# An S5 scan and a dilated local attention on one core: skip term and scan sums copied into PSUM by ScalarE, a pair level in the chunk scan, four taps per attention operation, and a new order of all work

## The chip, the core and the metric

The kernel runs on one core of one Trainium2 chip. The core has a matrix engine (TensorE, PE in the profile; its weight loads are shown apart as PEld), a vector engine (VectorE, DVE), an engine for copies and functions (ScalarE, ACT), a general one (GpSimd, POOL) and one that issues transfers (SyncE, SP). Matmuls read from the on-chip memory SBUF and write to, or add to, the accumulators in PSUM, eight banks of 512 float32 columns on 128 partitions in the way this kernel uses it. The time is the device time of one run in microseconds (us), the median of three runs.

## The reference

Two independent computations on sequences of S = 2048 positions and D = 448 channels; their results stand side by side in the output, 896 columns wide.

```python
# A: a diagonal state-space model (S5), complex state of 448
dt = jnp.exp(log_dt)
Lam_bar = jnp.exp(dt * Lam)
B_bar = ((Lam_bar - 1.0) / Lam)[:, None] * Bmat
Bu = jnp.einsum("bld,pd->blp", x + 0j, B_bar)
for t in range(L):
    h = Lam_bar[None, :] * h + Bu[:, t, :]
    hs.append(h)
y = 2.0 * jnp.einsum("blp,dp->bld", hseq, Cmat).real + x * Dskip[None, None, :]
# B: attention of 16 heads of 28 channels over 8 earlier positions, 2 apart
qkv = (x @ wqkv) ...                        # q, k, v
idx = pos[:, None] - jnp.arange(8) * 2      # positions below 0 are masked
logits = jnp.einsum("bhsd,bhswd->bhsw", q, kg) * scale
attn = _softmax(logits, axis=-1)
o = jnp.einsum("bhsw,bhswd->bhsd", attn, vg)
b = o.reshape(B, S, D) @ wo
```

Inputs and outputs are bfloat16.

## The kernel before

*Layout.* The 2048 positions are 128 chunks of T = 16. A chunk is a partition in position-major tiles and a column in transposed ones; a position j inside the chunk picks the tile.

*How the order is made.* Every piece of work is a unit (`P.add`) with an engine, a cost, the units it depends on, and the buffers it takes and gives back: two PSUM slots `W` of two banks, four slots `s` of one bank, three product buffers `PR`, and smaller rings. `Planner.run` could order them by cost and priority (`PRI`), but a list `ORDER` of 606 numbers replaces that: the units are issued in exactly that order. Each engine works through its own instructions in the order issued, and waits by semaphore where a unit depends on another engine.

*Part A, the scan.* The state is cut into 7 groups m of 128 rows (64 complex numbers as real and imaginary parts). For each group `scan` does the following, with up to three groups in flight:
- The inputs: matmuls of the transposed x with `Bcat` for the four residues i = j mod 4, each 512 columns (L1192, L1200). Residues 0 and 2 lie in the two banks of `scP`, 1 and 3 in `scb` tiles.
- ACT copies `scP` to `eP` (L1205). Matmuls with the power `L(1)` carry residue 0 to 1 and 2 to 3 (L1209), ACT copies `scb1` to `e1` (L1213), L(2) carries 1 to 3 (L1216), ACT copies (L1220), and L1224 to L1226 sum the four quarters of a chunk. Now the last 128 columns of `scb3` hold each chunk's total.
- The scan over 128 chunks, four levels. In each, ACT copies the 128 totals to `pbuf` (`evv`, L1229) and matmuls of 128 columns add the totals of earlier chunks (`l2`, L1234): 1, 2, 3 chunks back, then 4, 8, 12, then 16, 32, 48, then 64: ten matmuls. A fifth copy is the input of what follows.
- The way back: L1239 adds the carry to residue 3, ACT writes it to `h` (`ev3`, L1243). Residues 1, 0 and 2 left PSUM long ago, because their banks were wanted by the next group. So an identity matmul brings `e1` back into a PSUM slot (`back1`, L1252, in six groups), L1246 and L1247 add the carries, ACT copies it out (`ev1f`, L1258); two identity matmuls bring `eP` back (`back`, L1263, in five groups), carries are added, then L1269, and ACT copies it out (`evPf`, L1274). Where `PRI["h.."]` or `PRI["g.."]` is positive the banks are held instead: `eP` in groups 3 and 6, `e1` in group 6.

*Part A, the outputs.* For each pair of positions a `y_ps` slot `W` takes, per position, seven matmuls of 448 columns with `Ccat` (L1356). The skip term x * Dskip comes in two ways: for the first six pairs as four more matmuls per position (L1353) against a diagonal matrix `Dg`, which ACT builds at the start (L1101) from a transposed row of Dskip; for the last two pairs DVE multiplies positions 12 to 15 of x, loaded again, by Dskip (L1333) and adds them while it takes y out of PSUM (L1367). The first six pairs are taken out by ACT (L1365).

*Part B.* x is transposed partly by PE (L413) and partly by transfers; matmuls make q and k (L466, L473, L499), taken out by ACT and DVE (L201 to L207). DVE multiplies q with shifted k (L641, L645, into `prods`), PE sums over the channels of a head (L656, L662, `logits`). `softmax`: maximum on DVE (L684), subtracted by PE (L688), exponential on ACT (L694), sum by PE (L699), reciprocal and product on DVE (L703, L705), transposed by PE (L711) and copied by ACT in two halves (L716). Values come from L741 and lie in `vd`. Then `pv`, for four quarters of the positions in the order (1,1), (1,0), (0,1), (0,0): an operation on DVE multiplies two neighbouring taps of the values by their weights (L797, 3584 elements a partition, four of them), three adds (L800, or L812 in two parts in the last quarter) and a fold of the two halves (L809; the last quarter leaves it to PE). The partial sums live in `rb`, the products in `prods`. For three quarters a transfer transposes the result; the last one is transposed by PE (L849) and taken out by ACT (L854). `wo_ps` (L866) is the output projection, taken out in L201, and L205 for a part of one tile.

Of the kernel before, what the change touches and what calls it, by code (L numbers as in the profile page):

```python
# [34 lines left out]
KPOW = [1, 2, 4, 8, 12, 16, 32, 48, 64, 128, 192, 256, 512, 768, 1024]  # L35
# [4 lines left out]
WARM = 4  # L40
FILL = (1, 3)
PRI = dict(bm=-5.66, xa=2.77, cc=19.9, sc=2.9, ch=-27.35, bk=-0.56, v0=16.0, v1=-26.16, wo=-13.74, y=14.16, pw=-5.68, sm=13.48, lim=100.0, lim2=30.0, limv=70.0, qk=0.86, K11=-14.0, Q11=-13.0, K10=-12.0, Q10=-11.0, K01=-10.0, Q01=-9.0, K00=-8.0, Q00=-7.0, d3=10.94, h0=-1.0, g0=-1.0, h1=-1.0, g1=-1.0, h2=-1.0, g2=-1.0, h3=1.0, g3=-1.0, h4=-1.0, g4=-1.0, h5=-1.0, g5=-1.0, h6=1.0, g6=1.0, nd=4.0, xd=20.12)
ORDER = [
# [51 lines left out]
class Unit:  # L95
    __slots__ = ("eng", "cost", "fn", "deps", "prio", "acq", "rel", "lat", "end", "seq", "on", "until", "mode")


class Planner:


    def __init__(self, bufs):
        self.units = []
        self.free = {k: [0.0] * n for k, n in bufs.items()}

    def add(self, eng, cost, fn, deps=(), prio=0.0, acq=None, rel=None, lat=None, until=None,
            mode="f"):
        u = Unit()
        u.mode = mode
        u.eng = eng if isinstance(eng, tuple) else (eng,)  # L110
        u.cost = cost if isinstance(cost, tuple) else (cost,)
        u.fn, u.prio, u.rel, u.until = fn, prio, rel, until
        u.acq = () if acq is None else (acq,) if isinstance(acq, str) else acq
# [4 lines left out]
        return u  # L118

    def run(self):  # L120
        left = list(self.units)
        nwait = {id(u): len({id(d) for d in u.deps}) for u in left}
        users = {}
        for u in left:
            for d in {id(d): d for d in u.deps}.values():
                users.setdefault(id(d), []).append(u)
        ready = [u for u in left if not nwait[id(u)]]
        clock = {}
        order = []
        n = len(left)  # L130
        mode = "f"
        while len(order) < n:
            best = None
            for u in ready:
                if any(len(self.free[a]) < u.acq.count(a) for a in u.acq):
                    continue
                for eng, cost in zip(u.eng, u.cost):
# [3 lines left out]
                    for a in u.acq:  # L141
                        t = max(t, sorted(self.free[a])[u.acq.count(a) - 1])
                    if u.until is not None and eng == u.eng[-1] and t > u.until:
                        continue
                    key = (t, u.prio, u.seq, t)
                    if best is None or key < best[0]:
                        best = (key, u, eng, cost + (0.095 if eng == "PE" and u.mode != mode else 0.0))
            assert best, "no unit can start: %d left, waiting for %s" % (n - len(order), [(u.acq, u.fn.__qualname__) for u in ready])
            (_, _, _, t), u, eng, cost = best
            for a in u.acq:  # L150
                self.free[a].remove(min(self.free[a]))
# [5 lines left out]
            for a in (u.rel,) if isinstance(u.rel, str) else u.rel or ():  # L157
                self.free[a].append(u.end)
# [5 lines left out]
            order.append((t, u, cost))  # L164
        self.order = order
        if len(ORDER) == n:
            for i in ORDER:
                u = self.units[i % 1000]
                u.on = u.eng[i // 1000]
# [1317 lines left out]
```

## Time and profile before

The profile is of one execution. The trace's span is 140.4 us; what lies around it is in the runs' times but not in the span.

| what | us |
|---|---|
| median of 3 runs | 142.12 (142.12, 142.16, 141.61) |
| span of the profiled execution | 140.4 |
| PE busy | 134.9 |
| DVE busy | 120.9 |
| ACT busy | 93.6 |
| POOL busy | 21.1 |
| first product of q and k on DVE starts | 15.48 |
| first operation of `pv` on DVE starts | 66.98 |
| first y matmul on PE starts | 101.19 |
| last add of `pv` on DVE ends | 131.3 |
| last matmul ends | 137.0 |

The busy time of an engine is the time in which at least one of its instructions was running. Idle time on an engine counts only where something waits for that engine later. In the rows of groups, the first number is the busy time of the group, the second the mean length of one instruction in nanoseconds; matmuls overlap in that length, so the distance from one to the next is smaller and is read from the chain of waits, where "x4" is four matmuls in a row and the number before it their time together. The values in the slices of the clock are tenths of full speed.

### The profile page before, as it was taken

Reading aid. Unit: us, or ns where it says so; the run is one execution under the profiler, and the core shown is the slowest. Engines: PE = TensorE matmul, PEld = TensorE weight load, DVE = VectorE, ACT = ScalarE, POOL = GpSimd, SP = SyncE. Lnnn points to the kernel's source line nnn. Section 1 sums busy time; section 2 is a strip of 40 time slices with the busy share of each in tenths; the row PEclk is TensorE's granted clock in tenths of the full one; section 3 lists DMA queues with packets and bytes.
Section 4 is the critical chain, followed back from the end, with each engine's and each line's share of the span. In section 5 each row is a group of like instructions: output and inputs, shape, how many; then the busy total and the mean of one; then the engine's idle time right before and its main releaser. Section 6 shows DMA issues by size and latency. Waiting matters only on the chain.

```text
span 140.4 us, 2813 instructions
## 1 busy us (share of the span) xinstructions
PE 134.9 (96%) x1078; PEld 71.6 (51%) x1078; DVE 120.9 (86%) x128; ACT 93.6 (67%) x182; POOL 21.1 (15%) x68
## 2 busy tenths in 40 slices
PE   5999999999999999999999999999999999999990
PEld 1634333456554454666435554456655555555650
DVE  3245959999999989897998999999999999999931
ACT  3358879999765883578776789889873630551381
POOL 7374287000970000000000000000000000000000
PEclk9999999999999999999999999999999999999999
DMA  4965243996537616469999400600154155724044
GB/s 129 267 120 111 56 100 56 238 218 123 81 67 76 103 42 203 110 94 175 248 199 142 144 0 5 131 0 0 35 101 132 47 181 139 170 80 139 0 161 133
DMA packets 39390, 15.99 MB, mean 114 GB/s; under 512 B 31445, under 2 KB 38740, under 8 KB 39377
## 3 DMA queue, kind: packets, MB, share of 16 engines
q1 hardware_dynamic: 39314, 15.82, 50.6%
q8 instruction: 8, 0.13, 0.4%
q14 instruction: 5, 0.04, 0.1%
q10 hardware_dynamic: 63, 0.01, 0.0%
HBM read 4.27 MB, written 3.67 MB: 57 GB/s over the span
## 4 chain that ended last, share of the span: by engine, by line
PE 94%; DMA 2%; ACT 1%; issue 0%; DVE 0%; ACTq 0%
PE y_ps L1356 15%; PE qk_ps L466 12%; PE v_ps L741 9%; PE wo_ps L866 9%; PE scb L1192 7%; PE scP L1192 7%; PE logits L656 4%; PE scb L1234 3%; PE qk_ps L499 3%; PE qk_ps L473 2%; DMA ra<-in_B_x_dram 2%; PE scb L1209 2%; PE y_ps L1353 2%; PE scP L1200 2%; PE scP L1263 2%; PE pt_x L413 1%
## 5 line engine op out<-in xcount | busy, mean ns | idle before, releaser
L797 DVE TENSOR_TENSOR prods<-attn,vd 128x3584 bf16<-128x3584 bf16 x12 | 24.0, 2020 | 0.0
L641 DVE TENSOR_TENSOR prods<-qk 128x3072 bf16<-128x3072 bf16 (+1 forms) x17 | 22.8, 1379 | 1.0 <-PE logits L656 0.5
L800 DVE TENSOR_TENSOR rb<-rb,prods 128x3584 bf16<-128x3584 bf16 x11 | 22.2, 2022 | 0.1
L466 PE MATMUL qk_ps<-rb 128*128 128x512 bf16 x60 | 15.3, 386 | 0.0
L1356 PE MATMUL y_ps<-Ccat,qk 128*128 128x448 bf16 x64 | 14.9, 352 | 0.0
L866 PE MATMUL wo_ps<-wo_p,rb 128*128 128x448 bf16 x64 | 13.5, 352 | 0.0
L741 PE MATMUL v_ps<-rb 128*128 128x448 bf16 x64 | 13.1, 352 | 0.0
L1229 ACT CAST pbuf<-scb 128x128 bf16<-128x128 f32 x35 | 9.2, 272 | 4.9 <-PE scb L1234 4.3
L1192 PEld LDWEIGHTS <-Bcat 128*128 128x128 bf16 x84 | 7.6, 98 | 8.2 <-issue 1.9
L1356 PE MATMUL y_ps<-Ccat,h 128*128 128x448 bf16 x48 | 11.7, 353 | 0.0
L1365 ACT CAST qk<-y_ps 128x896 bf16<-128x896 f32 x6 | 5.4, 907 | 9.1 <-PE y_ps L1356 9.1
L201 ACT CAST qk<-wo_ps 128x448 bf16<-128x448 f32 (+1 forms) x16 | 8.3, 526 | 4.2 <-PE wo_ps L866 3.9
L1192 PE MATMUL scb<-xaT_sb,Bcat 128*128 128x512 bf16 x42 | 11.1, 380 | 0.0
L1192 PE MATMUL scP<-xaT_sb,Bcat 128*128 128x512 bf16 x42 | 10.9, 379 | 0.0
L201 ACT CAST qk<-qk_ps 128x512 bf16<-128x512 f32 (+2 forms) x14 | 7.8, 580 | 2.9 <-PE qk_ps L473 1.2
L203 ACT ACTIVATE qk<-qk_ps 128x512 bf16<-128x512 f32 (+1 forms) x16 | 9.3, 599 | 0.5 <-PE qk_ps L499 0.2
L466 PEld LDWEIGHTS <-rb 128*128 128x128 bf16 x60 | 5.8, 100 | 7.4 <-issue 1.2
L201 ACT CAST vd<-v_ps 128x448 bf16<-128x448 f32 x16 | 7.9, 542 | 2.5 <-PE v_ps L741 2.5
L1356 PEld LDWEIGHTS <-qk 128*128 128x128 bf16 x64 | 6.3, 98 | 5.8
L645 DVE TENSOR_TENSOR prods<-qk 128x768 bf16<-128x768 bf16 (+3 forms) x18 | 9.1, 569 | 0.1
L741 PEld LDWEIGHTS <-rb 128*128 128x128 bf16 x64 | 6.1, 98 | 5.3
L866 PEld LDWEIGHTS <-rb 128*128 128x128 bf16 x64 | 6.1, 98 | 5.0
(177 smaller groups left out, 251.9 us busy)
## 6 DMA issues: line engine op xcount, KB each, us to landing
out_dram<-qk SPq DMA_DIRECT2D x18, 112.0 KB, 1.7
out_dram<-qk SPq DMA_DIRECT2D x7, 224.0 KB, 2.2
vd<-vd SPq DMA_DIRECT2D x3, 392.0 KB
rb<-in_B_wqkv_dram SPq DMA_DIRECT2D x3, 336.0 KB
qk<-in_A_x_dram SPq DMA_DIRECT2D x1, 448.0 KB
ra<-in_A_B_re_dram SPq DMA_DIRECT2D x1, 392.0 KB
ra<-in_A_B_im_dram SPq DMA_DIRECT2D x1, 392.0 KB
rb<-in_A_C_re_dram SPq DMA_DIRECT2D x4, 98.0 KB
```

The source lines that it names most:

```text
L201: nc.scalar.copy(out, in_)
L203: nc.scalar.mul(out, in_, scale)
L466: nc.tensor.matmul(out(n), lhsT=w(n, full, k), rhs=self.xT[:, j:j + 4, k, :], start=(not rfirst and k == 1), stop=(rfirst and k == KT - 1) ...
L641: V.tensor_tensor(out.rearrange("p i j k q -> p i (j k) q"), qq.unsqueeze(1).to_broadcast([NCH, 2, 4 * nk, NCH]), bass.AP(kk.tensor, kk.of ...
L645: V.tensor_tensor(jk(out[:, i, a:e]), qq, kk, op=ALU.mult)
L741: nc.tensor.matmul(ps[:].rearrange("p h d -> p (h d)"), lhsT=self.xT[:, j, k, :], rhs=self.wv[:, k, :], start=(k == 0), stop=(k == KT - 1))
L797: V.tensor_tensor(tmp[i].rearrange("p (j d h) -> p j d h", j=8, d=DH), aa, self.vd[:, o:o + 8], op=ALU.mult)
L800: V.tensor_tensor(acc, acc, tmp[i], op=ALU.add)
L866: nc.tensor.matmul(ps[:], lhsT=o[:, kt, :], rhs=self.wo_p[:, KT * e + kt, :], start=(kt == 0), stop=(kt == KT - 1))
L1192: mt(box[i], lhsT=self.Bcat[:, k, m, :], rhs=self.xk(slice(i, None, 4), k), start=(i % 2 == 0 and k == 0), stop=False, **kw)
L1229: nc.scalar.copy(pb[:, dst, PAD:], box[3][:, 384:512])
L1356: nc.tensor.matmul(ps, lhsT=self.h[m][:, i, g * NCH:(g + 1) * NCH], rhs=self.Ccat[:, m, :], start=(m == 0 and not skip), stop=(m == NM - 1 ...
```

## The change

It has six parts.

1. *Skip term.* The matmuls with `Dg`, `Dg` itself and the transposed row of Dskip are gone. All of x is loaded again, in position-major form, in four transfers of four positions each, into the tile that held the transposed x (so after the last input matmul of the scan, `self.u_in`). DVE multiplies each by Dskip; ACT copies each pair into a y slot (`seed`) before the seven matmuls add to it; y is then a plain copy out, by ACT or DVE.
2. *Scan sums.* In `back1` and `back`, ACT copies `e1` and `eP` into the PSUM slot instead of identity matmuls, in the same groups (`FIN`: "seed" or "hold" for `eP` and `e1`).
3. *Pair level.* The chunk scan first adds each even chunk to the odd one after it, then runs three levels over the 64 odd chunks (2, 4, 6; 8, 16, 24; 32, 64, 96 chunks back), then adds the odd chunks to the even ones: 11 matmuls of 64 columns with five copies of 64 columns, and one of 128 at the end.
4. *Attention values.* An operation takes four taps (7168 elements): two multiplies and one add for a quarter. Both buffers, T1 and T2, lie in the product buffer `prods`, now 2 x 7168 long, so that the first multiply waits until the last logits have been summed.
5. *Softmax.* The reciprocal becomes a logarithm and an exponential on ACT; the transposed weights are copied by one operation instead of two.
6. *Front, buffers and order.* The k weights are loaded in two pieces; some copies change engines; the planner now knows which PSUM slot a unit takes (`Slot`), and keeps some for some uses; `ORDER` is a new list of 622 numbers, in which also some y and wo tiles are taken out by DVE after its last attention operation.

```diff
@@ scan: the way back
-            def back1(box=box):
-                t = self.psum.tile([NCH, 512], f32, name="scb1", tag="s")
-                box[1] = t[:]
-                mt(box[1], lhsT=cx.ident[:], rhs=box["e1"][:], start=True, stop=False, **kw)
+            def back1(eng, box=box, sl=sl, m1=m1):
+                box[1] = self.psum.tile([NCH, 512], f32, name="scb1", slot=sl["b1"])[:]
+                if eng == "ACT":
+                    nc.scalar.copy(box[1], box["e1"][:])
+                else:
+                    mt(box[1], lhsT=cx.ident[:], rhs=box["e1"][:], start=True, stop=False, **kw)
...
+            def back(eng, box=box, sl=sl, mP=mP):
+                box["P"] = self.psum.tile([NCH, 2, 512], f32, name="scP", slot=sl["P2"])
+                if eng == "ACT":
+                    nc.scalar.copy(box["P"][:], box["eP"][:])
@@ scan: the levels over the chunks
-            def evv(dst, box=box, pb=pb):
-                nc.scalar.copy(pb[:, dst, PAD:], box[3][:, 384:512])
+            tot = lambda a, d, box=box: box[3][:, 384 + a:512:d]
+            def evv(dst, a, d, pb=pb, tot=tot):
+                nc.scalar.copy(pb[:, dst, PAD:PAD + NCH // d], tot(a, d))
+            def l2(src, out, unit, ks, pb=pb, L=L, tot=tot):
+                for k in ks:
+                    sh = k if unit > 1 else 1 - out
+                    mt(tot(out, 2), lhsT=L(T * unit * k), rhs=pb[:, src, PAD - sh:PAD - sh + NCH // 2],
+                       start=False, stop=True, **kw)
...
-            for n, (unit, ks) in enumerate(((1, (1, 2, 3)), (4, (1, 2, 3)), (16, (1, 2, 3)), (64, (1,)))):
+            for n, (a, out, unit, ks) in enumerate(((0, 1, 1, (1,)), (1, 1, 2, (1, 2, 3)), (1, 1, 2, (4, 8, 12)),
+                                                    (1, 1, 2, (16, 32, 48)), (1, 0, 1, (1,)))):
@@ load_skip and outputs
+        for j in range(0, T, 4):
+            v = self.xT[:].rearrange("p j k q -> p j (k q)")[:, j:j + 4, 0:D]
+            def ld(v=v, j=j):
+                nc.sync.dma_start(v, xv[:, j:j + 4])
+            def mul(v=v):
+                nc.vector.tensor_tensor(v, v, box["d"].unsqueeze(1).to_broadcast([NCH, 4, D]), op=ALU.mult)
+            u = P.add("SP", dma(4 * D * 256), ld, self.u_in, 4, lat=3.0)
...
-                for k in range(KT if skip and m0 == 0 else 0):
-                    n = min(NCH, D - k * NCH)
-                    nc.tensor.matmul(ps[:, k * NCH:k * NCH + n], lhsT=self.xk(j + jj, k), rhs=self.Dg[:, k, 0:n],
-                                     start=(k == 0), stop=False, skip_group_check=True)
...
+            def seed(j=j, jb=jb):
+                jb["y"] = self.psum.tile([NCH, 2, 512], f32, name="y_ps", slot=jb["s"])
+                nc.scalar.copy(jb["y"][:, :, 0:D], self.xd[j])
@@ softmax
-            V.reciprocal(r[:, 0, :], box["sm"][:])
+            nc.scalar.activation(r[:, 0, :], box["sm"][:], ACT.Ln)
+            nc.scalar.activation(r[:, 0, :], r[:, 0, :], ACT.Exp, scale=-1.0)
@@ pv
+        T1, T2 = cx.pr[:, 0:4 * n1], cx.pr[:, 4 * n1:8 * n1]
...
+                V.tensor_tensor(out.rearrange("p (z j d h) -> p z j d h", z=2, j=8, d=DH),
+                                a.unsqueeze(3).to_broadcast([NCH, 2, 8, DH, H]),
+                                bass.AP(v.tensor, v.offset, [v.ap[0], [DIL * D, 2], [D, 8], [H, DH], [1, H]]),
+                                op=ALU.mult)
+            def add():
+                V.tensor_tensor(T1, T1, T2, op=ALU.add)
+            def fold(g=g):
+                V.tensor_tensor(T1[:, 0:2 * n1], T1[:, 0:2 * n1], T1[:, 2 * n1:4 * n1], op=ALU.add)
+                V.tensor_tensor(res[g], T1[:, 0:n1], T1[:, n1:2 * n1], op=ALU.add)
```

More of the change, by code (lines that the diff above doesn't have):

```diff
@@ L118, in add, with pick @@
         return u
+    def pick(self, u, t):
+        taken = []
+        for a in u.acq:
+            if isinstance(a, Slot) and a.i is not None:
+                continue
+            ring, need = (a, 0) if isinstance(a, str) else (a.ring, a.need)
+            c = [f for f in self.free[ring] if f[2] >= need and all((ring, f) != x[:2] for x in taken)]
+            if not c:
+                return None
+            taken.append((ring, min(c, key=lambda f: (max(f[0], t), f[2], f[1])), a))
+        return taken
     def run(self):
-        left = list(self.units)
-        nwait = {id(u): len({id(d) for d in u.deps}) for u in left}
+        nwait = {id(u): len({id(d) for d in u.deps}) for u in self.units}
         users = {}
-        for u in left:
+        for u in self.units:
             for d in {id(d): d for d in u.deps}.values():
                 users.setdefault(id(d), []).append(u)
[L127 to L132, printed above, removed]
+        ready = [u for u in self.units if not nwait[id(u)]]
+        clock, mode, n = {}, "f", len(self.units)
+        given = [(self.units[i % 1000], i // 1000) for i in ORDER] if len(ORDER) == n else None
+        for done in range(n):
             best = None
[L134 to L137, printed above, removed]
+            for u in ready if given is None else [given[done][0]]:
+                for k, (eng, cost) in enumerate(zip(u.eng, u.cost)):
+                    if given is not None and k != given[done][1]:
+                        continue
                     t = clock.get(eng, 0.0)
@@ L488, in banks @@
-            self.u_proj += us
-            return res
+                    mm(n, rows, 0)
+            dup = [self.u_xd[j], self.u_wd["Q" if tiles[1][0] == "Q" else "K" if one else "K01"]]
+            both = sl if one else sl[:1]
+            ua = P.add("PE", pe(3, 512), lambda: f(0), x + wd, prio, acq=sl[0])
+            ub = P.add("PE", pe(3, 512), lambda: f(1), x + wd, prio, acq=sl[1])
+            u = P.add("PE", pe(1, 512), rr, x + wd + dup, prio, acq=both, mode="r")
+            self.u_proj += [ua, ub, u]
@@ L672, in qk @@
                 prods.append(u)
[L673 removed]
+                u = P.add("PE", 0.33 if tp > 1 else 0.55, summ, [u] + sums[:1], -2, rel="PR", acq=self.lg_slot[b] if first else None, mode="c")
                 sums.append(u)
@@ new lines, in pv @@
+            after = [self.u_attn[b], *self.u_prod[0], *self.u_prod[1], *self.u_lg[0], *self.u_lg[1], *deps]
+            ms = []
+            for x in (1, 0):
+                o = j0 + 4 * r + 8 * x
+                dd = []
+                for p in range(o, o + 10):
+                    dd += self.u_vh[p] if p < HALO else [self.u_v[p - HALO]]
+                ms.append(P.add("DVE", vec2(4 * n1), lambda x=x, f=mul: f(x), [*dd, *after, last], prio - 0.1 * r))
+            last = P.add("DVE", vec2(4 * n1), add, ms, prio - 0.1 * r)
@@ L825, in pv @@
+            if g > 0:
+                last = P.add("DVE", vec2(2 * n1) + vec2(n1), fold, [last, *self.u_vm, *self.u_proj], prio - 0.1 * r)
+                lasts[r] = [last, last]
+            else:
+                l0 = P.add("DVE", vec2(n1), lambda: part(0), [last, *self.u_vm, *self.u_proj], prio)
+                l1 = last = P.add("DVE", vec2(n1), lambda: part(1), [l0], prio)
+                lasts[r] = [l0, l1]
             self.pv_last = last
@@ new lines, in back, with p2 @@
+            def back(eng, box=box, sl=sl, mP=mP):
+                box["P"] = self.psum.tile([NCH, 2, 512], f32, name="scP", slot=sl["P2"])
+                if eng == "ACT":
+                    nc.scalar.copy(box["P"][:], box["eP"][:])
+                else:
+                    for i in range(2):
+                        mt(box["P"][:, i, :], lhsT=cx.ident[:], rhs=box["eP"][:, i, :], start=True, stop=False, **kw)
+            def p2(box=box, sl=sl, mP=mP):
+                if mP == "add" and "P2" not in box:
+                    box["P"] = box["P2"] = self.psum.tile([NCH, 2, 512], f32, name="scP", slot=sl["P2"])
+                return box["P"]
@@ L1288, in scan @@
+            self.u_in += q
+            u = P.add("PE", pe(2, 512), s1, [eP, *q, u_pw], pc)
+            ue = u = P.add("ACT", act(512), ev1, [u], pc, rel=None if holde else sl[1])
             u = P.add("PE", pe(1, 512), s2, [u], pc)
@@ L1384, in outputs @@
-            eng, e = ("ACT", act) if skip else ("DVE", vec)
-            x = [] if skip else [self.u_xd[j]]
+            sl = jb["s"] = Slot("W", 1, 1)
+            pc = pe(7, 448)
+            hs = [self.u_h[:20], self.u_h[20:24], self.u_h[24:]]
+            first = [P.add("ACT", act(896), seed, [self.u_xd[j]], pr, acq=sl)]
+            x = []
+            if n < 3:
+                pc -= pe(2, 448)
+                us = [P.add("PE", pc, lambda f=y, i=i: f(i, m1=5), hs[0] + self.u_cc + first, pr, acq=sl) for i in range(2)]
+                v = P.add("PE", pe(2, 448), lambda f=y: (f(0, m0=5, m1=6), f(1, m0=5, m1=6)), us + hs[1], pr)
+                v = P.add("PE", pe(2, 448), lambda f=y: (f(0, m0=6), f(1, m0=6)), [v] + hs[2], pr)
+                us = [v, v]
+            else:
+                us = [P.add("PE", pc, lambda f=y, i=i: f(i), self.u_h + self.u_cc + first, pr, acq=sl) for i in range(2)]
```

560 lines of the change are left out of this document (248 added, 312 removed), and 56 rows, old and new, of the table ORDER.

## The prediction

> **What bounds the kernel now.** I read the engine sums and the clock row first, then the chain that ended last, then busy time by stage, then the groups of rows, the waits, and the timeline of the end.
>
> ```profile
> PE 134.9 (96%) x1078; PEld 71.6 (51%) x1078; DVE 120.9 (86%) x128; ACT 93.6 (67%) x182; POOL 21.1 (15%) x68
> PEclk9999999999999999999999999999999999999999
> ...
> PE 94%; DMA 2%; ACT 1%; issue 0%; DVE 0%; ACTq 0%
> ```
>
> TensorE (PE) holds the chain at a clock of 0.9 or more in every slice. But PE was given enough work in the right order to fill every gap, so the chain may pass along it while another engine sets the pace. The stages (columns: stage, length, then busy time of each engine):
>
> ```profile
> 15.50:50.50 35.00, 35.00 (x343) 18.03 (x342) 32.28 (x37) 28.92 (x54) 13.10 (x19) 1.00 0.60 112
> 50.50:67.00 16.50, 16.50 (x193) 9.67 (x190) 14.56 (x22) 10.77 (x26) 0.00 (x0) 1.00 0.60 131
> 67.00:101.20 34.20, 33.73 (x242) 17.81 (x241) 33.65 (x21) 28.19 (x63) 0.00 (x0) 1.00 0.41 90
> 101.20:131.40 30.20, 30.20 (x200) 16.80 (x198) 29.94 (x19) 12.26 (x19) 0.00 (x0) 1.00 0.43 115
> 131.40:140.40 9.00, 5.61 (x53) 3.53 (x50) 3.45 (x5) 4.55 (x9) 0.00 (x0) 1.00 0.35 115
> ```
>
> From 67 on VectorE (DVE) is as full as PE: 33.65 of 34.20 and 29.94 of 30.20 us. Its last attention add ends at 131.33, and only then come the last transposes and output products:
>
> ```profile
> 129.24 2.09 DVE L812 TENSOR_TENSOR rb<-rb,prods 128x1792 bf16<-128x1792 bf16 x2
> ...
> 131.44 0.89 PE pt_o L849 x16
> 132.34 1.51 PE wo_ps L866 x8
> 133.85 0.89 PE pt_o L849 x16
> 134.74 2.28 PE wo_ps L866 x12
> ```
>
> So two queues are near bound: DVE from its first product (15.48) to 131.33, then a tail of 9.07 us to 140.4; and PE everywhere. A change that relieves PE alone gains the tail and little else. ScalarE (ACT) has room only on average: 28.19 of 34.20 in the stage of the scan.
>
> **The change, part by part.** Prices are from these rows and from lengths in the chain of waits.
>
> ```profile
> L797 DVE TENSOR_TENSOR prods<-attn,vd 128x3584 bf16<-128x3584 bf16 x12 | 24.0, 2020 | 0.0
> L1229 ACT CAST pbuf<-scb 128x128 bf16<-128x128 f32 x35 | 9.2, 272 | 4.9 <-PE scb L1234 4.3
> L1274 ACT CAST qk<-scP 128x1024 bf16<-128x1024 f32 x4 | 4.1, 1032 | 0.6 <-PE scP L1269 0.6
> L1258 ACT CAST qk<-scb 128x512 bf16<-128x512 f32 x4 | 2.4, 595 | 0.3 <-PE scb L1247 0.3
> L703 DVE RECIPROCAL rsum<-sm_ps 128x128 f32<-128x128 f32 x2 | 1.9, 958 | 1.2 <-PE sm_ps L699 1.2
> 101.19 0.20 PE y_ps L1353 x4
> 66.42 0.43 PE scP L1263 x2
> 66.85 0.22 PE scb L1252
> 62.75 0.17 PE scb L1234 x3
> ```
>
> *Skip term.* PE loses 12 groups of four matmuls at 0.20: −2.4 us. ACT gains 8 copies of 896 columns into PSUM. No row of before has ACT writing PSUM; the nearest are the y eviction of the same shape the other way (907 ns) and a copy inside SBUF (64x512 in 617, dearer than the 512 eviction at 595). I take 907, so +7.3 us; they fall where ACT is idle 18 of 30 us, and without that cover they would delay each y by 0.9. The four Dg scalings (4 x 400 ns) go. DVE gets four multiplies of 1792 at 1.09 (one before, behind the last add): with the overlap of 0.08 that independent neighbours show, +4.0 us ahead of the end of attention. SP issues four loads of 448 KB where one was; they overwrite the transposed x and so wait for the last scan input. At the 200 to 250 GB/s of the busy slices they take 7 to 9 us. The multiplies sit inside the attention queue of DVE: if a load is late, everything behind waits, 0 to 2.5 us.
>
> *Scan copies.* PE loses 5 x 0.43 + 6 x 0.22 = 3.5 us; ACT gains 5 x 1.03 + 6 x 0.60 = 8.8 us, in the stage where it has 6.0 of 34.2 us left.
>
> *Pair level.* Before, 10 matmuls of 128 columns a group at 57 ns (0.17 for three): 7 x 10 x 0.057 = 4.0 us. After, 77 of 64 columns. The 64-column ones among the skip matmuls must fit in 0.20 − 3 x 0.057, or 0.03; the upper bound is 0.057, when loading weights sets the pitch. That is 2.3 to 4.4, and I take the middle, 3.3: −0.7 us (−1.7 to +0.4). ACT takes 42 short copies instead of 35, smaller ones: +0 to 2 us; each hop is also one more wait of ACT on PE like those 4.3 us.
> The Trainium skill ("TensorE: Matmul & The Clock Gate", section "Back-to-back issue gap") gives about 81 ns for a matmul of 128 columns in a stream of weight loads and matmuls. The trace differs: 57. By the page's figure for both, 77 x 81 against 70 x 81 would be a loss of 0.6 us.
>
> *Attention values.* Sixteen multiplies and eleven adds of 3584, three folds and two parts of 1792 become eight multiplies and four adds of 7168, three folds of 3584 and five of 1792. The step from 1792 (1.09) to 3584 (2.02) is 0.93, so 7168 is 2.02 + 1.86 = 3.88. Busy: 27 x 2.02 + 5 x 1.09 = 60.0 against 12 x 3.88 + 3 x 2.02 + 5 x 1.09 = 58.1. Part of each start was already overlapped, so by start-to-start times −1.0 us (bounds −0.7 and −2.0). New is a wait: the sums now lie in the buffer of the logit products, so the first big multiply waits for the last logits on PE, 1 to 2.3 us in place of the 0.99 that the maximum waits for them today; behind it in DVE's queue is all the attention work.
>
> *Softmax.* Two reciprocals of 0.958 and their 1.2 us of waits leave DVE (−2.1 us by start-to-start times, −1.2 idle). ACT takes Ln and Exp on 128x128, some 0.3 each by the 272 ns row; the table loads stay at three if both functions share a table, otherwise 1.28 more each.
>
> *Front.* Two more loads on SP, issued in 0.43 to 0.58 each, stand ahead of the x transposes (1.3 each), so the first product comes 0 to 1.05 later; I take 0.8. Three query and key evictions leave DVE and a weight copy comes to it: −1.3; other small ones −0.4.
>
> *Order.* All 622 units are in a new order. PE carries four more groups of wo before the first y (4 x 0.76).
>
> *Sums.* PE: −2.4 − 3.5 − 0.7 = −6.6 us. DVE from the end of its first product (16.36) to the end of attention: 131.33 − 16.36 = 114.97, of which 4.3 idle and 110.6 work (start to start). After: 110.6 + 4.0 − 2.1 − 1.0 − 1.3 − 0.4 = 109.8. Idle: 4.3 − 1.2 for the reciprocals, −1.5 for what a lighter PE hands over sooner, + 0.9 net for the new waits: 2.5 (0 to 6). So attention ends at 16.36 + 0.8 + 109.8 + 2.5 = 129.5. Behind it PE has the rest of the transposes, two y matmuls and four groups of wo, 26 x 0.057 + 2 x 0.19 + 4 x 0.76 = 4.9, started 0.15 later, then one eviction of 0.54 and the 2.5 from there to the end: 8.1; 7.9 if part starts on the first half. Span 137.4. The median was 142.12 with a span of 140.4, so 1.7 us lie outside it: **139.1 us**.
>
> Check by PE: its work ahead of the first y hardly changes (−6.6 is spread over both sides, and wo moves forward: 94.7 to 94.4), from there to its end 35.9 becomes 29.8. First y at 101 to 105 (before 101.2) plus 29.8, 1 of stalls and 3.2 gives 135 to 139: PE is no longer last unless the scan slips.
>
> **The rivals.**
> *A, PE's gain is paid nearly in full.* DVE's idle shrinks to 0 or 1: attention ends at 127 to 128, span 135 to 136, median 136.6 to 137.6. For it: from 67 to 131 DVE already idles only 0.8 us of 64.4. Against: four new waits on that queue.
> *B, the waits eat it.* Logits 2.3, loads 2.5, key pieces 1.4 on top of 1: idle 6, attention at 133.0 and the sum 142.6, no change that can be told. A difference within 0.5% (0.7 us) is about what a measurement of this kernel can't tell from none.
> *C, slower: ACT becomes the bound of the scan.* Its idle time from 50.5 to 101.2 is 50.7 − 10.8 − 28.2 = 11.7 us, nearly all of it waits for PE inside the scan's chain, as L1229 shows. If it can't be used, the 8.8 us of copies lengthen the stage one for one; PE's last scan group, m=6, with nothing beside it, stalls first. First y at 101.2 + 8.8 = 110.0, end at 110.0 + 29.8 + 1 + 3.2 = 144.0, median 145.7. Half of it, 105.6, is still faster (141.3); it decides from a first y at 107 on (median 142.8). For it: the rows of ACT in the scan. Against: most copies read data that is ready long before, and can fill gaps.
> *D, a copied seed is not kept by the matmuls' accumulation, so the change does not do what it says:* the time would be the same as forecast; no case of its own.
>
> **How the numbers follow.** Forecast (137.5 to 141.2) 0.55; A 0.17; B 0.15; C 0.13. The likeliest gives 139.1. Low end: A's middle less a little, 136.0; high end takes in B and a mild C: 143.0. Faster by over 0.5% (below 141.4) 0.72, the forecast and A; same 0.13; slower (above 142.8) 0.15.
>
> **What would show it.** No L1263, L1252 and L1353 matmuls, PE busy near 128; ACT near 105 busy with 1024 copies into scP near 1.0 and y seeds near 0.9; DVE work between first product and attention's end near 110, with waits at the first big multiply (on PE) and at the skip multiplies (on DMA); three table loads; a tail near 8. I am wrong if DVE idles over 5 us there, if ACT copies into PSUM take far from 1.0 and 0.6, if 64-column matmuls are above 57 ns, or if the first y starts after 107.

## The result

The change made the kernel slower: 146.08 us against 142.03 for the kernel before on the same chip, a ratio of 1.030 (95% interval 1.026 to 1.033). The span grew from 140.4 to 143.9 us. The forecast was 139.1.

The page of the changed kernel, sums and chain of waits:

```profile
PE 131.1 (91%) x1020; PEld 67.9 (47%) x1020; DVE 122.5 (85%) x118; ACT 105.9 (74%) x207; POOL 22.6 (16%) x68
...
PE 51%; ACT 12%; DMA 6%; issue 2%; SPq 0%; ACTq 0%
```

TensorE is busy 3.8 us less, ScalarE 12.3 us more, and ScalarE now holds 12% of the chain, against 1% before. (The view follows this chain back only to 37.84 us, 71% of the span, so its shares can't be set beside the 94% of before one by one.) By stages of the same bounds as before the change:

```profile
15.50:50.50 35.00, 32.68 (x320) 16.53 (x317) 31.73 (x36) 29.04 (x52) 13.90 (x20) 1.00 0.63 112
50.50:67.00 16.50, 16.50 (x197) 9.43 (x194) 14.53 (x17) 11.61 (x27) 0.00 (x0) 1.00 0.14 37
67.00:101.20 34.20, 32.10 (x228) 16.81 (x226) 34.06 (x17) 31.37 (x76) 0.00 (x0) 1.00 0.68 158
101.20:131.40 30.20, 29.03 (x159) 14.88 (x157) 30.03 (x13) 22.32 (x34) 0.00 (x0) 1.00 0.47 125
131.40:143.90 12.50, 8.25 (x67) 4.92 (x64) 4.75 (x7) 4.13 (x8) 0.00 (x0) 1.00 0.36 115
```

TensorE now has holes in the front (2.3 us), in the scan (2.1) and in the y stage (1.2), where before they came to 0.5 in all. What it lost there comes back at the end: 8.25 us of matmuls lie behind 131.4, 5.61 before. VectorE is as full as it was, 34.06 of 34.20 and 30.03 of 30.20, and ends no sooner. Its timeline in the changed kernel (the bracket is the idle time before, and what ended it):

```profile
32.25 0.22 DVE L583 COPY qk<-qk 128x24 bf16<-128x24 bf16 x1 [2.54 <-ACT qk L227]
...
64.79 3.89 DVE L817 TENSOR_TENSOR prods<-attn,vd 128x7168 bf16<-128x7168 bf16 x1 [1.97 <-PE logits L684]
...
129.82 2.09 DVE L832 TENSOR_TENSOR prods<-prods 128x1792 bf16<-128x1792 bf16 x2
```

Attention ends at 131.91 (before 131.33), and 12.0 us follow instead of 9.07. The end of the chain of waits shows what fills them:

```profile
128.94 3.03 PE y_ps L1382 x16
131.97 0.76 PE wo_ps L890 x4
132.72 1.70 PE y_ps L1382 x9
134.43 0.45 PE pt_o L873 x8
...
136.48 0.89 PE pt_o L873 x16
137.38 2.28 PE wo_ps L890 x12
```

Eleven y matmuls, which need nothing of the last attention result, are still to be done after it, because the first y matmul started at 108.58 instead of 101.03. (Both are starts from the timeline. The 101.19 given for the kernel before is the same matmul in the chain of waits, where a piece begins when the one ahead of it ends.) Before, no y matmul was left when attention ended.

A balance over TensorE makes the sizes plain. For each matmul I take the usual distance from its start to the next one's as its work (57 ns for 128 columns and for the 64 columns of the levels, 28 for the 64-column remainders of the skip term, 189 for 448, 215 for 512; where several run side by side, at most 100 or 216), and call the rest lost:

| us | work | lost 0 to 35 | 35 to 67 | 67 to 101.2 | 101.2 to 131.4 | first y | attention ends |
|---|---|---|---|---|---|---|---|
| before | 126.4 | 5.6 | 1.6 | 2.1 | 0.0 | 101.0 | 131.3 |
| after | 120.8 | 7.8 | 1.9 | 5.8 | 2.0 | 108.6 | 131.9 |

Work fell by 5.6 us, but 8.2 us of new losses came in, and TensorE's end moved by the difference, from 137.0 to 139.7. (The trace of a run can lack a few matmul records. The counts of these two, 1078 and 1020, differ by just what the code changed.)

### The profile page after: what moved, and what is told of

Same layout as the page of the kernel before. It is cut to its first block, busy times and chain, and to the rows that moved or that the text cites. A ratio compares the mean times of both kernels' runs of the same rounds, so it can differ in the third digit from the quotient of the medians.

```text
span 143.9 us, 2721 instructions
## 1 busy us (share of the span) xinstructions
PE 131.1 (91%) x1020; PEld 67.9 (47%) x1020; DVE 122.5 (85%) x118; ACT 105.9 (74%) x207; POOL 22.6 (16%) x68
## 4 chain that ended last, share of the span: by engine, by line
PE 51%; ACT 12%; DMA 6%; issue 2%; SPq 0%; ACTq 0%
PE y_ps L1382 9%; PE v_ps L769 8%; PE scb L1201 7%; PE scP L1201 7%; PE wo_ps L890 5%; ACT qk L227 4%; DMA out_dram<-qk 3%; DMA xaT_sb<-in_A_x_dram 3%; PE logits L678 3%; PE scb L1245 2%; PE scb L1218 2%; ACT y_ps L1394 1%; PE pt_o L873 1%; ACT pbuf L1240 1%; PE logits L684 1%
## 5 line engine op out<-in xcount | busy, mean ns | idle before, releaser
L817 DVE TENSOR_TENSOR prods<-attn,vd 128x7168 bf16<-128x7168 bf16 x8 | 30.9, 3885 | 2.0 <-PE logits L684 2.0
L492 PE MATMUL qk_ps<-rb 128*128 128x512 bf16 (+1 forms) x80 | 18.0, 380 | 3.0 <-ACT qk L227 1.2
L823 DVE TENSOR_TENSOR prods<-prods 128x7168 bf16<-128x7168 bf16 x4 | 15.6, 3890 | 0.1
L1201 PE MATMUL scP<-xaT_sb,Bcat 128*128 128x512 bf16 (+1 forms) x56 | 13.8, 382 | 0.1
L1201 PE MATMUL scb<-xaT_sb,Bcat 128*128 128x512 bf16 (+1 forms) x56 | 13.9, 382 | 0.0
L1201 PEld LDWEIGHTS <-Bcat 128*128 128x128 bf16 (+1 forms) x112 | 8.8, 99 | 10.6 <-issue 4.5
L492 PEld LDWEIGHTS <-rb 128*128 128x128 bf16 (+1 forms) x80 | 6.4, 97 | 12.4 <-issue 5.3
L1240 ACT CAST pbuf<-scb 128x64 bf16<-128x64 f32 (+1 forms) x42 | 9.3, 237 | 3.8 <-PE scb L1245 2.3
L1245 PE MATMUL scb<-pbuf,pw 128*128 128x64 bf16 x77 | 9.6, 236 | 1.4 <-ACT pbuf L1240 1.0
L890 PEld LDWEIGHTS <-rb 128*128 128x128 bf16 x64 | 5.9, 97 | 5.5 <-issue 0.4
```

The lines of the kernel that those rows point to most:

```text
L492: nc.tensor.matmul(out(n), lhsT=w(n, rows, k), rhs=self.xT[rows, j:j + 4, k, :], start=n not in begun, stop=True, skip_group_check=True)
L817: V.tensor_tensor(out.rearrange("p (z j d h) -> p z j d h", z=2, j=8, d=DH), a.unsqueeze(3).to_broadcast([NCH, 2, 8, DH, H]), bass.AP(v.te ...
L823: V.tensor_tensor(T1, T1, T2, op=ALU.add)
L890: nc.tensor.matmul(ps[:], lhsT=o[:, kt, :], rhs=self.wo_p[:, KT * e + kt, :], start=(kt == 0), stop=(kt == KT - 1))
L1201: mt(ps(i), lhsT=lhsT, rhs=rhs, start=i not in begun, stop=True, **kw)
L1240: nc.scalar.copy(pb[:, dst, PAD:PAD + NCH // d], tot(a, d))
```

## The experiments

Two questions: what makes TensorE lose 8.2 us more, and what the saved 5.6 us were worth at all. Ratios are against the kernel before, run on the same chip; the changed kernel stands at 1.030.

| run | us | ratio (95%) | first y | attention ends |
|---|---|---|---|---|
| fin_pe | 146.65 | 1.030 (1.024 to 1.036) | 110.95 | 133.6 |
| no_skip | 145.03 | 1.018 (1.012 to 1.024) | 109.46 | 130.1 |
| pair_old | 147.40 | 1.035 (1.030 to 1.041) | 108.75 | 132.4 |
| logits_early | 147.73 | 1.037 (1.031 to 1.043) | 109.90 | 133.1 |
| front_swap | 145.50 | 1.026 (1.021 to 1.030) | 107.67 | 131.0 |
| front_both | 144.43 | 1.018 (1.013 to 1.022) | 107.20 | 130.5 |
| front_outs | 143.74 | 1.014 (1.007 to 1.021) | 107.54 | 130.9 |
| fin_none | 145.20 | 1.024 (1.020 to 1.028) | 108.10 | 132.2 |
| hops_free | 145.84 | 1.026 (1.020 to 1.032) | 108.75 | 133.0 |
| hops_fin | 143.31 | 1.012 (1.010 to 1.014) | 106.39 | 131.9 |
| after_lean | 141.36 | 0.999 (0.996 to 1.002) | 104.96 | 130.5 |
| before_fin | 148.88 | 1.051 (1.044 to 1.058) | 107.24 | 132.6 |
| before_lean | 141.24 | 0.997 (0.994 to 1.000) | 99.16 | 130.6 |
| before_dve | 141.77 | 1.001 (0.999 to 1.004) | 100.64 | 129.0 |
| before_both | 138.89 | 0.981 (0.979 to 0.983) | 99.12 | 128.5 |

### One part taken back

**fin_pe**, **no_skip** and **pair_old** each take one part out of the changed kernel; **logits_early** moves the wait at 64.79. (In these excerpts a line in words stands for several lines of code, and three dots for what is left out.)

```diff
-FIN = (("seed", "seed"), ("seed", "seed"), ...    # fin_pe: identity matmuls again
+FIN = (("pe", "pe"), ("pe", "pe"), ...
-                nc.scalar.copy(jb["y"][:, :, 0:D], self.xd[j])      # no_skip: no loads, no
+                (left out, with the loads and multiplies)            # multiplies, no seeds
-  levels: pairs, then 64 columns three times, then pairs             # pair_old
+  levels of 128 columns, four as before
-ORDER = [... 451, ... 258, ... 195, 191, 193, ...]                   # logits_early
+ORDER = [... 195, 191, 451, ... 258, 193, ...]
```

> The scan sums go back to identity matmuls (the eleven copies of eP and e1 into PSUM become 16 matmuls of 512 columns), all else as in the changed kernel, same order. ACT theory (the scan stage is bound by ScalarE, so the first y comes at 108.6): ACT loses 9.0 us there, PE gains 3.5, the first y comes at 104 to 106, the time falls to 142 to 144.5. Rival, PE and DVE set the pace and ACT is only busy: the first y does not come earlier, the time is 146 to 149.

> Leaves the skip term out of y: no second load of x, no multiplies, no copies into the y slots; the first of the seven matmuls starts the sum. ACT theory: the copies it loses (7.3 us) lie behind the scan, so the first y is 0 to 1.5 us earlier; DVE loses 4.2 us ahead of the end of attention (131.8 to 127.6), but PE's late y work still sets the end: 143 to 145. Rival, the late load and the copies into y hold the first y: it comes 3 us or more earlier and the time is 139 to 142.

> The chunk scan goes back to four levels of 128 columns (70 matmuls, 35 copies), all else as in the changed kernel. If the pair level costs what the rows say (77 matmuls at 57 ns against 70, copies 9.6 us in sum on both sides): PE 0.4 us less, ACT the same, the time 145 to 146.3. If the extra hop between ACT and PE in each group is what delays the scan: 1 to 3 us faster, 143 to 145.

> Only the order: the last three sums of logits are issued on PE 1.5 to 3 us earlier, ahead of a v projection and a scan step, so that the first big multiply on DVE need not wait 2.0 us for them. ACT theory: attention ends up to 1.9 us earlier, the first y and the end do not move by more than 0.5 us: 145.5 to 146.5. Rival, DVE sets the end: 144 to 144.8.

None brings the time back, and two forecasts missed altogether: pair_old and logits_early came out slower than either of their theories. With the identity matmuls the first y is even later (110.95): in this order they stand at places chosen for ScalarE, so the run mixes two things. Without the skip term the first y is later too, by 0.9; the loads and seeds do not hold it. They are not free, though: without them attention ends 1.8 us sooner and the time falls by 1.2%, to 145.03, which is just above the forecast of 143 to 145. With four levels of 128 columns it is where it was, and the interval overlaps that of the changed kernel. Moving the logits ahead turned VectorE's wait of 1.97 us on TensorE into one of 2.95 on a value tile that ScalarE evicts later. So none of these parts is the cause by itself in the place that it has. The four taps per operation and the softmax were not taken back one by one.

### The front and the outputs

The waits of TensorE in the changed kernel (what waits, for what, us in all, times, longest):

```profile
PE qk_ps L492 <- ACT qk L227: 1.2, 1, 1.2
PE scb L1245 <- ACT pbuf L1240: 1.0, 2, 0.5
PE qk_ps L492 <- ACT qk L229: 0.9, 2, 0.6
PE y_ps L1382 <- ACT y_ps L1394: 0.9, 1, 0.9
PE qk_ps L492 <- DMA rb<-in_B_wqkv_dram: 0.9, 1, 0.9
```

The first, at 30.79, is a matter of order alone: the copy out of one bank of a `qk_ps` tile (unit 113) is issued ahead of the matmuls into its other bank (unit 111), and these then wait for it. VectorE's 2.54 us at 32.25 end with the copy that follows those matmuls. The last is the second piece of the K weights.

```diff
-ORDER = [... 113, ... 111 ...]                                       # front_swap
+ORDER = [... 111, 113, ...]
-        wload(D, D + 2 * NCH)                                        # front_both: and this
-        wload(D + 2 * NCH, 2 * D)
+        wload(D, 2 * D)
-ORDER = [... 497 ... 521, 515, 500 ... 512 ... 518 ...]              # front_outs: and this
+ORDER = [... 497, 512, 515, 521 ... 500, 517, 518 ...]
```

> Only the order, in the front: the second group of q matmuls into a two-bank PSUM tile is issued ahead of ACT's copy out of the tile's first bank, as in the kernel before; in the changed kernel the copy is issued first and PE waits for it (PE idle before the matmul at 30.79). Theory F (the front's order costs time that nothing later absorbs): that wait of 1.3 us is gone, DVE's wait of 2.5 us at 32.25 falls to about 1.2, the time falls by 1.0 to 1.6, to 144.5 to 145.1. Rival, later waits absorb it: 145.7 to 146.4.

> As front_swap, and the k weights are loaded in one piece as in the kernel before (two transfers fewer ahead of the x transposes). Theory F: PE's wait of 1.1 us for the second piece at 8.2 goes too, and the x transposes are issued 1.1 earlier; another 0.5 to 1.1 us, 143.6 to 144.6. Rival: no more than front_swap.

> front_both (one load of the K weights, the K matmul issued ahead of the copy) and besides, on the queue of SyncE, the output transfers of four out-projection results issued right after their evictions instead of 6 to 25 us later; nothing else. In front_both ScalarE waits for free output buffers, a seed is late by it, and the y matmuls wait 1.6 us for that seed at 117.5. Theory O (these waits are on the path that sets the end): they go, time 142.6 to 143.6 against 144.4 of front_both. Rival: another seed or eviction takes their place, time 144.0 to 144.9.

The swap by itself came between the two expectations and can't be told from the changed kernel with certainty. TensorE's wait is gone from the list, but VectorE's wait shrinks only from 2.54 to 1.75 us, where 1.2 was expected:

```profile
31.32 0.22 DVE L553 COPY qk<-qk 128x24 bf16<-128x24 bf16 x1 [1.75 <-ACT qk L197]
```

The copy that it waits for now stands behind others in ScalarE's queue, which is busy without a pause from 27.5 to 33 us. With the one load it is 1.2% better than the changed kernel, as theory F said: attention ends 1.4 us sooner and the first y starts 1.4 sooner. In front_both the waits for outputs are then the largest that are left:

```profile
PE y_ps L1351 <- ACT y_ps L1363: 1.4, 1, 1.4
```

With the outputs issued early that wait is gone and the span falls from 142.6 to 141.5; by the runs the step is about 0.4%. The time lies between the two expectations, and the intervals overlap. Together the three are 1.6% or 2.3 us.

### The scan

In the old order first. **before_fin** puts ScalarE's copies where the kernel before has its identity matmuls; **fin_none** leaves them out of the changed kernel (ScalarE 9.0 us lighter).

```diff
-                mt(box[1], lhsT=cx.ident[:], rhs=box["e1"][:], start=True, ...)   # before_fin
+                nc.scalar.copy(box[1], box["e1"][:])
-                nc.scalar.copy(box["P"][:], box["eP"][:])                         # fin_none
+                pass
```

> The kernel before, with one part of the change alone: the sixteen identity matmuls become eleven ACT copies into PSUM, in the same places of the order. (A copied bank may be overwritten instead of added to here, which the time does not see.) ACT theory: ACT gets 9.0 us more in a stage with 6.0 us left from 67 to 101; the first y comes at 101 to 104 although PE has 3.5 us less to do, the time is 141.5 to 144. Rival, ACT absorbs the copies: first y at 98, attention on DVE sets the end, 140 to 141.5.

> Leaves out the sums of the way back: neither ACT copies nor identity matmuls put eP and e1 back into PSUM, the carries start the sum; all else and the order as in the changed kernel. ACT theory (its queue in the scan delays PE): ACT loses 9.0 us, PE's waits on ACT between 67 and 108 fall from about 4 us to under 2, the first y comes at 105 to 106.5, the time is 143 to 144.8. Rival, the length of the chain and the issue order make PE wait, not ACT's load: first y at 108 to 109, 145.3 to 146.4.

Both expectations failed for before_fin: it lost 7 us. Its waits of TensorE say where:

```profile
PE scb L1246 <- ACT scb L1252: 4.3, 4, 1.3
PE scP L1246 <- ACT scP L1262: 3.1, 4, 1.3
```

Where an identity matmul stood in TensorE's own queue, a copy is a round trip, and the eight waits for it make 7.4 us. In the changed kernel these copies are issued early, and TensorE waits 0.2 us for them. Yet fin_none gained only 0.6%. So they cost more than nothing, but they are not what holds the scan alone. The chain of waits of the changed kernel from 77 to 85 shows the other candidate:

```profile
78.77 0.49 ACT scb L1265
79.26 0.27 ACT pbuf L1240
79.53 0.43 ACT eG L1229
79.96 0.92 ACT eP L1214
80.87 0.12 ACT pbuf L1240
80.99 0.49 ACT h L1254
81.48 0.12 ACT pbuf L1240
81.60 0.53 ACT scP L1283
82.12 0.26 issue
82.39 0.26 ACT pbuf L1240
```

For 7.4 us, from 77.3 to 84.8, the chain stays on ScalarE: the short copies of the levels (L1240) stand in its queue between long ones, and TensorE can't start a level before its short copy. ScalarE holds the chain again right ahead of the first y. From 101.66 to 108.5 its copies follow each other almost without a pause: those out of the last scan groups, three evictions of wo results, and the first seed at the end:

```profile
105.63 1.04 ACT L227 CAST qk<-wo_ps 128x448 bf16<-128x448 f32 x2
106.47 1.11 ACT L227 CAST qk<-scP 128x1024 bf16<-128x1024 f32 x1
107.62 0.91 ACT L1394 CAST y_ps<-xaT_sb 128x896 f32<-128x896 bf16 x1
```

What the wo evictions cost there was not tested. **hops_free** cuts the exchange between the levels and keeps the work.

```diff
-                nc.scalar.copy(pb[:, dst, PAD:PAD + NCH // d], tot(a, d))
+                nc.scalar.copy(pb[:, dst, PAD:PAD + NCH // d], pb[:, dst, 0:PAD] if d > 1 else tot(a, d))
-                    mt(tot(out, 2), lhsT=..., rhs=pb[:, src, PAD - sh:PAD - sh + NCH // 2],
+                    mt(tot(out, 2), lhsT=..., rhs=pb[:, src, 0:PAD],
```

> The changed kernel with the data exchange of the five short levels cut: each matmul of the levels reads a block of zeros that nobody writes, each copy of the levels copies zeros, so TensorE does not wait for ScalarE between levels nor ScalarE for TensorE. Both engines issue the same instructions of the same sizes in the same order. It leaves out the sums over the pairs inside a chunk. Theory L (TensorE's lost time in the scan is the exchange itself: matmul, copy, matmul, with too little other work left in between): TensorE loses at most 3 us between 67 and 101 us (5.8 in the changed kernel, 2.0 before), first y matmul at 104 to 106 instead of 108.6, time 142 to 143.7. Rival A (ScalarE has too much to do there, whoever waits for it): its amount is the same, so first y stays at 108 or later and the time at 145 to 146.5.

> The changed kernel with the data exchange of the five short levels cut (hops_free) and the 14 copies of sums into PSUM left out (fin_none), each of which alone left the first y matmul where it was. Theory B (two limits lie one behind the other in the scan, the exchange and ScalarE's amount, and each takes over when the other goes): first y at 104 to 106, TensorE loses at most 3 us between 67 and 101, time 142 to 143.5. Rival R (neither: TensorE's own order, or VectorE, holds the scan): first y at 107.5 or later, 144.3 to 146.

(The text for hops_fin speaks of 14 copies of sums; there are eleven.) hops_free fell on the side of rival A: 145.84, first y at 108.75. (Its short copies took 262 ns instead of 229, which gives ScalarE some 1 us more.) But A alone does not do either: in fin_none, without the copies, the first y came only 0.5 us sooner. The busy times from 77 to 85 (columns as in the stages above) for the changed kernel, hops_free, fin_none, and hops_fin with both:

```profile
77.00:85.00 8.00, 6.94 (x50) 3.46 (x48) 7.97 (x7) 7.73 (x20) 0.00 (x0) 1.00 0.86 163
```
```profile
77.00:85.00 8.00, 7.02 (x48) 3.57 (x47) 7.97 (x6) 7.76 (x21) 0.00 (x0) 1.00 0.81 150
```
```profile
77.00:85.00 8.00, 7.17 (x51) 3.58 (x50) 7.97 (x6) 6.20 (x17) 0.00 (x0) 1.00 0.83 157
```
```profile
77.00:85.00 8.00, 7.58 (x55) 3.80 (x53) 7.97 (x7) 5.85 (x17) 0.00 (x0) 1.00 0.84 160
```

TensorE idles 1.06 us there. When only the exchange is cut it still idles 0.98, with ScalarE as full as before (7.76 of 8). When only the copies go it idles 0.83, although ScalarE has 1.8 us free: TensorE waits level by level. With both gone it is 0.42. Over the run the single gains are 0.4% and 0.6%, with intervals that overlap that of the changed kernel, and the joint one is a clear 1.8%: two limits stand one behind the other. The first y came at 106.39, a little later than the 104 to 106 expected, and 4.1 us are still lost from 67 to 101.2 where at most 3 were expected; about 2.5 us of these stand ahead of matmuls that wait for ScalarE's longer copies, those to `e`, `eG` and `h`. No run takes those away.

### What the saving was worth

**before_lean** only takes away TensorE's work in the old order, **before_dve** takes 4.0 us from VectorE, **before_both** does both. **after_lean** is hops_fin and front_outs in one.

```diff
-                mt(box[1], lhsT=cx.ident[:], rhs=box["e1"][:], start=True, ...)   # before_lean: and the
-                    mt(box["P"][:, i, :], lhsT=cx.ident[:], rhs=box["eP"][:, i, :], ...)
-                for k in range(KT if skip and m0 == 0 else 0):                    # 48 skip matmuls
-                        add(n)                                                    # before_dve
+                        if n == 2 or 2 * b + r < 2:
+                            add(n)
```

> The kernel before, in its own order, with the matmuls left out that the change replaces, and with nothing in their place: no skip term in y (its 28 small matmuls) and no identity matmuls that bring the sums back in the scan (the outputs lack both). TensorE loses about 5.9 us of work, ScalarE and VectorE keep theirs. Theory P (TensorE is the bound of the kernel before, all the way): 136 to 137.5, first y at 97 to 98. Theory V (VectorE's attention ends at 131.3 all the same and at least 7.9 us follow): 140 to 141.5, with first y at 97 to 98.5 and TensorE idle at the end. Theory S (work taken out of the scan turns into waits there): first y not before 99.5, TensorE loses at least 2 us more between 67 and 101, 140 to 142.

> The kernel before without two of the eleven long sums in PV on VectorE (two instructions of 2.02 us each; the output lacks those terms); TensorE and ScalarE as before. before_lean took 5.9 us of work from TensorE and gained under 1 us. Theory T (TensorE and VectorE end together in the kernel before, so that neither saving counts alone): 141 to 142.2, no gain. Rival W (VectorE alone sets the end, TensorE's share of 94% of the chain notwithstanding): 137.3 to 139.

> before_lean and before_dve in one: TensorE 5.9 us and VectorE 4.0 us lighter (skip term, back sums and two PV sums left out), in the order of the kernel before. Theory T (the two engines tie): now the time falls, to 136.5 to 138.5. Rival X (something else, ScalarE or a fixed end, holds the kernel at 139 or more): 139.5 to 141.5.

> hops_fin and front_outs in one: exchange cut, sums' copies left out, one load of the K weights, the K matmul ahead of the copy, the four outputs issued early. Theory B: 140 to 141.5, and no lower, since VectorE's attention ends at about 130.5 and some 8.5 us follow. Rival R: 142.5 to 143.8, as front_outs.

(The text for before_lean speaks of 28 skip matmuls; there are 48.) Its page and stages:

```profile
PE 48%; DVE 41%; issue 6%; DMA 2%; ACT 0%; DVEq 0%; ACTq 0%
```
```profile
67.00:101.20 34.20, 33.18 (x235) 17.52 (x234) 33.96 (x21) 29.07 (x65) 0.00 (x0) 1.00 0.37 83
101.20:131.40 30.20, 27.39 (x155) 14.12 (x154) 29.97 (x18) 10.92 (x17) 0.00 (x0) 1.00 0.45 115
131.40:139.50 8.10, 4.72 (x37) 2.65 (x34) 2.76 (x5) 4.18 (x9) 0.00 (x0) 1.00 0.40 130
```

5.8 us of TensorE's work went (16 matmuls at 215 ns, 36 at 57 and 12 at 28) and the time fell by 0.4 us, or not at all. TensorE now idles 2.8 us between 101.2 and 131.4 and VectorE, full throughout, takes over 41% of the chain; its attention ends at 130.65 instead of 131.33. Four us less on VectorE alone gained nothing either, and there TensorE keeps 94% of the chain:

```profile
PE 94%; POOL 2%; ACT 1%; issue 1%; DVE 0%; POOLq 0%; ACTq 0%
```

Both together gained 1.9% (2.8 us; theory T had said 3.2 at least, so the time lies between T and rival X). A joint gain where neither gains alone means that the two engines tie in the kernel before, which is theory T with V for before_lean. And after_lean, with front, outputs and scan relieved, lands at 141.36, as theory B said: level with before_lean, no lower. Its attention ends at 130.5 and 9.0 us follow, much as in the kernel before. VectorE is busy there for 64.1 of the 64.4 us from 67 to 131.4, which fits VectorE as the limit. It is not shown: the chain of that run, followed back to 36.42, has 2% of VectorE, and its work on VectorE was not taken away in a trial. No complete version beat the kernel before; a version that makes VectorE and TensorE lighter in the old order, without copies in the scan, was not tried.

## Why the prediction was wrong

*What held.* The prices: copies into PSUM, the big products, and the two functions of the softmax:

```profile
L1394 ACT CAST y_ps<-xaT_sb 128x896 f32<-128x896 bf16 x8 | 7.3, 912 | 0.2
...
L1283 ACT CAST scP<-eP 128x1024 f32<-128x1024 bf16 x5 | 5.4, 1085 | 0.0
...
L1265 ACT CAST scb<-e 128x512 f32<-128x512 bf16 x6 | 3.6, 603 | 0.0
...
L728 ACT ACTIVATE rsum<-rsum 128x128 f32<-128x128 f32 x2 | 0.6, 310 | 0.1
L727 ACT ACTIVATE rsum<-sm_ps 128x128 f32<-128x128 f32 x2 | 0.6, 290 | 0.0
```

Forecast were 907, 1.03 and 0.60, 0.3 each. The products took 3885 ns against 3.88; the first one waited 1.97 us (1 to 2.3 forecast); the skip multiplies did not wait for their loads. TensorE's work fell by 5.6 us against 6.6: the pair level was mis-sized, at 57 ns for a matmul of 64 columns it costs 0.4 us more than the old one and does not save 0.7. That is the upper bound that the prediction had kept. The Trainium skill ("TensorE: Matmul & The Clock Gate", section "Back-to-back issue gap") lets the weight load count at small widths, and by its figure for both widths more matmuls meant a loss; the loss is borne out in the levels, the 81 ns is not, it is 57.

The span was to be 137.4 and is 143.9. Of these 6.5 us, 2.4 lie ahead of the end of attention (129.5 against 131.9) and 4.1 in the tail behind it (7.9 against 12.0).

*First failed step: "2.5 (0 to 6)" us of idle time on VectorE, so attention at 129.5.* By the same count (waits in brackets) it is 2.54 + 0.39 + 1.97 = 4.9. The waits for the reciprocal went as forecast, and the logits' came as forecast; the 2.54 at 32.25 was not in the sum at all. Part of it comes from the order of two units: swapping them left 1.75, and one load of the K weights besides left 1.61. The rest hangs on ScalarE's copies in the front; what makes them late stays open. The new order of all work holds both, and it was priced at nothing beyond four groups of wo on TensorE. The work came to 110.6 instead of 109.8, and the front's extra 0.8 did not show (first product ends at 16.37, before 16.36): 16.37 + 110.6 + 4.9 = 131.9.

*Second failed step: the tail of 7.9 and the check "First y at 101 to 105".* The check said that TensorE would not be last "unless the scan slips". It slipped to 108.58, and 108.6 + 29.8 of work + about 1.2 of waits gives TensorE's end at 139.7. The prediction had itself the case: rival C, with 110.0 and 145.7, named ScalarE's idle time in the scan as unusable. Its direction and size are right (146.08), at a chance of 0.13. Its mechanism is half of it: hops_fin shows that ScalarE's amount and the exchange both hold the scan, and 2.3 us are won back by mending the front and the outputs, which C did not name.

*Third: the ceiling.* "A change that relieves PE alone gains the tail and little else" was written, and then a gain of 1.2 us in the tail and 1.8 on VectorE was booked. before_lean is the measurement of that sentence in the old order: 0.4 us for 5.8 us of TensorE's work. Within the 1.8, a lighter TensorE that hands over sooner was booked at 1.5 us of VectorE's idle time; in before_lean VectorE's attention ended 0.7 sooner.

## What to carry to other kernels

A share of 94% on one engine's chain does not say that relieving it pays: if a second engine is as full from the middle to the end, leave out the first one's work in a trial before building its replacement, and take the gain that this shows as the most that relieving it can bring in that order. A matmul replaced by a copy on another engine is a round trip where it stands in a tight chain; it must be issued early, and then its amount lands on the engine whose short copies the chain waits for. When two limits lie one behind the other, taking each away alone shows little; try them together before dropping either.

## What the runs showed of the hardware

In the chain of waits three matmuls of 64 columns in a level take 0.17 us, 57 ns each, as three of 128 columns did before:

```profile
61.24 0.17 PE scb L1245 x3
```

So in the levels the columns saved were not time saved. (By start times the first matmul of a level is followed 28 ns sooner than that, and the matmul behind the level 27 ns later than usual, so nothing is left.) That is no rule for the width: the 64-column matmul that ended each group of the skip term in the kernel before took 28 ns. What makes the difference is open.

Copies by ScalarE between SBUF and PSUM took much the same either way: 912 ns out of SBUF into PSUM and 907 the other way for 896 columns, 603 and 587 for 512, 1085 and 1027 for 1024. The Trainium skill ("ScalarE: Activation LUTs", section "Step-by-step: what each stage is for") calls PSUM the faster destination of the two. These copies can't decide it, because their sources differ too, and the source counts: in hops_free a short copy of 64 columns took 262 ns out of SBUF, against 229 out of PSUM.
